# Tiles 4 and 5 of an attention turned by transposing DMAs and multiplied with the values in the banks of the gates

## The chip, the cores and the metric

The kernel runs on one core of one Trainium2 chip. The metric is the device time of one execution in microseconds (us). Before the change the median of 3 runs is 861.51 us (860.49 to 862.71).

## What is computed

```python
def reference(q, k, v, w_gate, w_val, w_out, w2_in, w2_out):
    # attention; keys and values are averaged in groups of 8 (576 -> 72)
    s = q @ mean8(k).T / sqrt(64)              # 4 batches, 8 heads, 576 queries
    x = softmax(s) @ mean8(v)                  # put together: 2304 x 512
    # gated layer, width 1536
    x = (sigmoid(x @ w_gate) * (x @ w_val)) @ w_out
    # second layer, width 2048
    h = x @ w2_in
    return (h * tanh(softplus(h))) @ w2_out    # 2304 x 512
```

All inputs are 64-bit floats in HBM. The kernel turns them into 32-bit floats itself, and multiplies matrices with three products of rounded halves (high by high, high by low, low by high).

## The kernel before, in words

**Blocks and parts.** The 2304 tokens are cut into blocks of 512, 512, 512 and 768. The first block of the gated layer, about the stretch from 55 to 140 us, is the one that matters here. Its loop runs over 12 slices of 128 of the hidden width (f = 0 to 11), and each slice has three *parts*: part 3f is the gate product (tile `pg`, L604 to L608), part 3f + 1 the value product (tile `pv`, same lines), part 3f + 2 the output product of the slice before (tiles `acc`, L123 to L125). So part 19 is the value product of slice 6, part 24 the gate product of slice 8, part 25 its value product, and part 26 the output product of slice 7.

**Banks.** `pg` and `pv` take turns in a pool of two PSUM banks ("mm"). A gate's bank is free when ScalarE has read it with a tanh (L954); a value's bank is free when VectorE has read it with `sg = (tanh + 1) * pv` (L960). Attention has another pool of two banks ("at").

**The table of small work.** Between two parts stand words of a table, START, written out by hand: the words after part k are recorded behind part k, on whatever engine they use. An engine takes its instructions in that order. The words after the block's parts do two things.
- They prepare the attention of the *next* block (tiles 4 to 7, 128 tokens each): scores (`m`), minimum (`M`), exponential (`X`, L465), normalising (`N`, L478 to L481), turning the weights of 128 tokens by 72 keys to 72 by 128 (8 heads), and the product with the pooled values.
- They convert the weights of the gated layer, 36 of them (24 of the gates and values, 12 of the output, `wo`): load (`raw_next`, L682), a scaling on ScalarE (`C`, L277), two bit operations on VectorE (`A`, L286 and L291), the rounded high half on ScalarE (`B`, L115) and the low half on GpSimd or VectorE (L310). Each `A` also issues the next load on SyncE.

**Two ways to turn a tile.** Tiles 4 and 5 are turned on TensorE: `t` makes 4 transposes in an "at" bank (L490), `c` copies them to SBUF on ScalarE or VectorE (L115 or L117), `p` multiplies with the values (L500), `h` and `l` split the product into halves (L514, L516), each of them for half of the heads at a time. Tiles 6 and later take the other way: `Y` clears a buffer `planes` on GpSimd (L547), `y` splits the 32-bit weights into two planes of 16-bit words on ScalarE (L553), a transposing DMA on SyncE's queue turns them (L559, tile `turned`), `j` joins the words again (four copies of ScalarE, L115), and `O` and `o` do the product with the values for all heads in one bank, with one rounding on ScalarE (L531) and one subtraction on VectorE (L532).

**Buffers.** `planes`, `turned` and the raw 64-bit weights of `wo` share one pool of three buffers ("raw"). The raw weights of gates and values have buffers of their own.

Of the kernel before, what the change touches and what calls it, by code (L numbers as in the profile page):

```python
# [26 lines left out]
E0.1 L1.0 B:a E1.1 C:a | A B:a A C:a |  |  | G:p B:a C:a K1.0:a A L1.2 C:a J1.0 B:a | A B:a G:p A  # L27
C:a | B:a C:a | C:a L1.3 A K1.1:a J1.1 B:a K1.2:a Z1.0:v | A A C:a J1.2 B:a B:a G:v Z1.1:v J1.3
K1.3:a C:a | A Z1.3:p | C:a A Z1.2:p | G:p B:d A B:a J1.4 C:a A m4.0 B:a | C:a | B:a M4.0 Q6 | A
m4.1 C:a | Z1.4:p X4.0 M4.1 G:v B:a F1 X4.1 C:a N4:v A C:a A H1 A B:a B:a | B:a C:a | A C:a t4.0 B:a  # L30
C:a | t4.1 | G:v A c4.0:a c4.1:v | A B:a | p4.0 p4.1 h4.1 h4.0 C:a G:v l4.0 l4.1 A B:a C:a B:a C:a A
| m5.0 A C:a B:a M5.0 m5.1 M5.1 X5.0 B:a Q7 X5.1 N5:p | A C:a B:a | G:v A | C:a B:d C:a | G:v t5.0
C:a A A c5.0:a | t5.1 B:a C:a c5.1:v A | B:a p5.0 A p5.1 B:a h5.0 l5.0 h5.1 l5.1 |  | m6.0 C:a M6.0
m6.1 A M6.1 X6.0 X6.1 G:v B:d C:a N6:v Y6 | A y6 B:a C:a m7.0 M7.0 m7.1 M7.1 X7.0:v X7.1:v | N7:v Y7
y7 A B:e G:p Q8 | B:a | Q9 j6.0 j6.1 | j7.0 j7.1:v G:v L2.0 L2.1 | O6 O7 o6 o7 | d m8.0 M8.0 m8.1
M8.1 | X8.0 X8.1 Q10 K2.0:v K2.1:v L2.2 L2.3 | r:a N8:v Y8 | s d y8 | b K2.2:v K2.3:v U2.0 U2.1 S0 |
r:a D0 | s d m9.0 M9.0 m9.1 M9.1 z0 | j8.0 b X9.0 X9.1 Q11 V2.0:p V2.1:v U2.2 U2.3 | j8.1 r:a N9:v
Y9 | s d y9 V2.2:p V2.3:v U2.4 U2.5 S1 | b D1 | r:a V2.4:p V2.5:v U2.6 U2.7 z1 | s d m10.0 M10.0
m10.1 M10.1 | j9.0 b X10.0 X10.1 Q12 V2.6:p V2.7:v | j9.1 r:a N10:v Y10 S2 | s d y10 D2 | O8 O9 b o8
o9 z2 | r:a | s d m11.0 M11.0 m11.1 M11.1 | j10.0 b X11.0 X11.1 Q13 S3 | j10.1 r:a N11:v Y11 L3.0  # L40
L3.1 D3 | s d y11 z3 | b | r:a K3.0:v K3.1:v L3.2 L3.3 | s d m12.0 M12.0 m12.1 M12.1 S4 | j11.0 b
X12.0 X12.1 Q14 D4 | j11.1 r:a N12:v Y12 K3.2:v K3.3:v U3.0 U3.1 z4 | s d y12 | b | O10 m13.0 M13.0
o10 m13.1 M13.1 O11 o11 r:a V3.0:p V3.1:v U3.2 U3.3 | s d | j12.0 b X13.0 X13.1 Q15 V3.2:p V3.3:v
U3.4 U3.5 S5 | j12.1 r:a N13:v Y13 D5 | s d y13 V3.4:p V3.5:v U3.6 U3.7 z5 | b S6 | r:a V3.6:p
V3.7:v D6 | j13.0 s d m14.0 M14.0 m14.1 M14.1 z6 | j13.1 b X14.0 X14.1 Q16 | r:a N14:v Y14 | s d y14
S7 | O12 O13 b D7 | r:a z7 | s d m15.0 M15.0 m15.1 M15.1 | j14.0 b X15.0 X15.1 Q17 | j14.1 r:a N15:v
Y15 S8 | s d y15 D8 | b z8 | r:a | s d m16.0 M16.0 m16.1 M16.1 | j15.0 b X16.0 X16.1 S9 | j15.1 r:a
N16:v Y16 D9 | s d y16 z9 | O14 O15 b | r:a | s d m17.0 M17.0 m17.1 M17.1 S10 | j16.0 b X17.0 X17.1
D10 | j16.1 r:a N17:v Y17 z10 | s d y17 | b | r:a S11 | s d D11 | j17.0 b z11 | j17.1 r:a | s d |
O16 O17 b | r:a x0.0 x0.1 x0.2 x0.3 x0.4 | s d x1.0 x1.1 x1.2 x1.3 x1.4 | b x0.5 x0.6 x0.7 x0.8 x0.9  # L50
x0.10 | r:a x1.5 x1.6 x1.7 x1.8 x1.9 x1.10 | s x0.11 | b x1.11 | x0.12 x0.13
"""

BIAS = 2.0**-112
# [3 lines left out]
def tile_pooled_attention_moe_mish(  # L58
# [14 lines left out]
    B, _, NPAIR, S = kt.shape  # L73
# [36 lines left out]
    def f32(ap):  # L110
        return ap.bitcast(F32)
# [15 lines left out]
    with tc.manual_schedule():  # L127
# [119 lines left out]
        with ExitStack() as actx:  # L247
# [10 lines left out]
            raw_q, scale_q, half_q = [], [], []  # L258
# [3 lines left out]
            def load_raw(src, eng=nc.sync, t=None):  # L262
                if t is None:
                    t = pa.tile([128, 512, 2], U32, tag="raw", name="raw", bufs=3)
                eng.dma_start(out=t.rearrange("p c w -> p (c w)"), in_=src.bitcast(U32))
                raw_q.append(t)

            def conv_scale(eng):

                raw = raw_q.pop(0)
                hi = f32(raw[:, :, 1])
                c = bits_at.pop(0) if bits_at else pa.tile([128, 512], U32, tag="cv", name="cv", bufs=3)
                if eng is nc.scalar:
                    eng.activation(out=f32(c), in_=hi, func=AF.Prelu, scale=BIAS, alpha=-(2.0**32))  # L277
                else:
                    eng.tensor_scalar_mul(f32(c), hi, BIAS)
                scale_q.append((raw, c, eng is nc.scalar))  # L280
# [149 lines left out]
            def ps_tile(tag, name):  # L430
                pool = {"mm": ps_mm, "at": ps_at}.get(tag, ps_acc)
                return pool.tile([128, 512], F32, tag=tag, name=name)
# [62 lines left out]
            def att_pv(T, g, tag="at", ps=None):  # L495
                ps = ps_tile(tag, "pv")[:, 0:256] if ps is None else ps
                for t0, n, b in segs(128 * T, 128):
                    for h in range(4 * g, 4 * g + 4):
                        p0, c0 = D * (h % 2), 128 * (h // 2 - 2 * g) + t0
                        nc.tensor.matmul(  # L500
                            ps[p0 : p0 + D, c0 : c0 + n],
                            vb_t[b][:, h, :],
                            pt_t[T][:, h, t0 : t0 + n],
                            start=True,
                            stop=True,
                        )
                pv_t[T, g] = ps.rearrange("p (a t) -> p a t", a=2)
# [9 lines left out]

            def att_values_out(T, j):

                ps = ps_tile("mm" if T in (10, 11) else "at", "pv")  # L520
                for g in range(2):
                    att_pv(T, g, ps=ps[:, 256 * g : 256 * g + 256])
                    del pv_t[T, g]
                t0 = 128 * T - blocks[j][0]
                if j == NBLK - 1:
                    c, t0 = divmod(t0, NG)
                    nc.scalar.copy(out=xs_t[0][:, :, c, t0 : t0 + 128], in_=ps.rearrange("p (k t) -> p k t", k=KD))
                    return lambda: None
                h, lo = (x[:, :, t0 : t0 + 128] for x in x_t[j % 2])
                ps = ps.rearrange("p (k t) -> p k t", k=KD)  # L530
                nc.scalar.copy(out=h, in_=ps)  # L531
                return lambda: nc.vector.tensor_sub(out=lo, in0=ps, in1=f32(h))  # L532
# [108 lines left out]
            with tc.tile_pool(name="pst", bufs=1, reuse_waits="tile") as pst:  # L641
# [29 lines left out]
                order = [("w", 0), ("w", 1), ("w", 2), ("w", 3), ("o", 0)]  # L671
                for f in range(NF):
                    if f + 2 < NF:
                        order += [("w", 2 * f + 4), ("w", 2 * f + 5)]
                    if f + 1 < NF:
                        order.append(("o", f + 1))
                pos = dict.fromkeys("lcab", 0)
                places = [
                    wpool.tile([128, 512, 2], U32, tag="w", name=f"wr{i}", bufs=2 * NF) for i in range(2 * NF)
                ]  # L680

                def raw_next(eng=nc.sync):  # L682
                    if pos["l"] < len(order):
                        kind, i = order[pos["l"]]
                        if kind == "o":
                            load_raw(wo[i], eng)
                        else:
                            load_raw((wg, wv)[i % 2][i // 2], eng, places[i])
                        pos["l"] += 1

                def scale_next(eng):
                    if pos["c"] < len(order):
                        conv_scale(eng)
                        pos["c"] += 1

# [219 lines left out]
            for j, (o, n) in enumerate(blocks[:-1]):  # L915
# [29 lines left out]
                for f in range(NF):  # L945
                    pg, pv = ((pre[f, nm] if j == 0 and f < 2 else None) for nm in "gv")
# [10 lines left out]
                    if pv is None:  # L957
                        pv = ps_mm.tile([128, 512], F32, tag="mm", name="pv")
# [76 lines left out]
            V, A = nc.vector, nc.scalar  # L1035
            for f in range(NF):
# [3 lines left out]
                a = pg_pool.tile([128, NG], F32, tag="sg", name="a", bufs=2)  # L1040
                u, v = (pg_pool.tile([128, NG], F32, tag="gh", name=t, bufs=2) for t in "uv")
                y = pg_pool.tile([128, NG], F32, tag="gl", name="y", bufs=2)

                def product(k):

                    pool, tag = banks1[k % 4]
                    ps = pool.tile([128, 512], F32, tag=tag, name=f"q{k}")
                    wt, c0 = where[k]
                    for kk in range(2):
                        xh, xl = pr[k, kk]  # L1050
                        mm3(ps[:, :NG], wt, slice(c0 + 128 * kk, c0 + 128 * kk + 128), xh, xl, kk == 0, kk == 1)
                    return ps[:, :NG]
# [10 lines left out]
                p5 = product(5)  # L1063
# [22 lines left out]
                p4 = product(4)  # L1086
# [96 lines left out]
        with ExitStack() as bctx:  # L1183
            pb = bctx.enter_context(tc.tile_pool(name="pb", bufs=1, reuse_waits="tile"))
            late = {f: pb.tile([128, NG], F32, name=f"g2_{f}") for f in range(6, NF2)}
            u0, v, a6, a7 = (pb.tile([128, NG], F32, name=t) for t in ("u", "v", "a6", "a7"))
# [57 lines left out]
            V, A, P = nc.vector, nc.scalar, nc.gpsimd  # L1244
# [75 lines left out]
            for p in range(NPR):  # L1320
                o = 2 * NG * p
# [5 lines left out]
                for i in range(NFP):  # L1327
# [12 lines left out]
                    a = a_at[i] if wino else a7  # L1340
# [170 lines left out]
                for j, (k, i) in enumerate(jobs[:-2]):  # L1511
# [7 lines left out]
                    if j in (8, 19):  # L1519
                        h = (8, 19).index(j)  # L1520
                        for t in range(NTG):
                            x = ob[t][:, half[h]]
# [100 lines left out]
```

## Time and profile before

| | |
|---|---|
| median of 3 runs | 861.51 us (860.49 to 862.71) |
| the profiled execution | 861.3 us |
| its span, first to last instruction | 859.3 us |
| mean granted clock of TensorE | 1.000 |
| TensorE busy | 850.5 us |
| VectorE, ScalarE, GpSimd busy | 627.6, 450.2, 143.9 us |

The profiled execution took 0.2 us less than the median, and 2 us of it lie outside the span. TensorE is busy nearly throughout; what another engine does counts where TensorE waits for it.

### The profile page before, as it was taken

Reading aid. Unit: us, or ns where it says so; the run is one execution under the profiler, and the core shown is the slowest. Engines: PE = TensorE matmul, PEld = TensorE weight load, DVE = VectorE, ACT = ScalarE, POOL = GpSimd, SP = SyncE. Lnnn points to the kernel's source line nnn. Section 1 sums busy time; section 2 is a strip of 40 time slices with the busy share of each in tenths; the row PEclk is TensorE's granted clock in tenths of the full one; section 3 lists DMA queues with packets and bytes.
Section 4 is the critical chain, followed back from the end, with each engine's and each line's share of the span. In section 5 each row is a group of like instructions: output and inputs, shape, how many; then the busy total and the mean of one; then the engine's idle time right before and its main releaser. Section 6 shows DMA issues by size and latency. Waiting matters only on the chain.

```text
span 859.3 us, 14411 instructions
## 1 busy us (share of the span) xinstructions
PE 850.5 (99%) x5044; PEld 780.3 (91%) x5044; DVE 627.6 (73%) x1181; ACT 450.2 (52%) x1067; POOL 143.9 (17%) x160
## 2 busy tenths in 40 slices
PE   8999999999999999999999999999999999999998
PEld 7887888888888888999999999998899999999998
DVE  6989774776675654778988977765577788566784
ACT  7656766554566544444454655555333466334454
POOL 3566431110120000010010024553000000000000
PEclk9999999999999999999999999999999999999999
DMA  9898537998889877165677789987598579776353
GB/s 339 308 309 270 157 114 235 285 265 248 274 211 290 233 213 258 62 221 196 226 241 235 277 316 330 349 286 270 180 293 293 184 224 315 258 238 226 120 191 99
DMA packets 117347, 207.02 MB, mean 241 GB/s; under 512 B 34972, under 2 KB 67740, under 8 KB 117276
## 3 DMA queue, kind: packets, MB, share of 16 engines
q1 hardware_dynamic: 116268, 204.12, 72.6%
q10 hardware_dynamic: 1008, 2.00, 0.7%
q8 instruction: 40, 0.66, 0.3%
q14 instruction: 31, 0.25, 0.1%
HBM read 143.80 MB, written 55.98 MB: 233 GB/s over the span
## 4 chain that ended last, share of the span: by engine, by line
PE 85%; DVE 6%; DMA 4%; ACT 3%; issue 2%; SPq 0%; ACTq 0%; DVEq 0%
PE acc L1218 8%; PE p L123 7%; PE p L125 7%; PE p L124 7%; PE x L1300 7%; PE acc L123 4%; PE acc L1300 4%; PE acc L125 4%; PE acc L124 4%; PE q L125 3%; PE q L123 3%; PE q L124 3%; PE pv L604 3%; PE pv L605 3%; PE pv L608 3%; PE pg L604 3%
## 5 line engine op out<-in xcount | busy, mean ns | idle before, releaser
L123 PE MATMUL p<-top,w2s 128*128 128x384 f32 x216 | 72.3, 335 | 0.0
L125 PE MATMUL p<-top,w2s 128*128 128x384 f32 x216 | 72.3, 335 | 0.0
L124 PE MATMUL p<-top,w2s 128*128 128x384 f32 x216 | 72.3, 335 | 0.0
L1218 PE MATMUL acc<-w,g 128*128 128x512 f32 x288 | 67.1, 390 | 0.0
L1218 PEld LDWEIGHTS acc<-w,g 128*128 128x128 f32 x288 | 53.9, 188 | 10.9
L123 PE MATMUL acc<-gh,wo 128*128 128x512 f32 x144 | 57.1, 396 | 0.0
L965 ACT CAST gh<-sg 128x512 fp32r<-128x512 f32 x36 | 22.3, 620 | 65.8 <-DVE sg L960 65.8
L124 PE MATMUL acc<-gl,wo 128*128 128x512 f32 x144 | 56.3, 391 | 0.0
L125 PE MATMUL acc<-gh,wo 128*128 128x512 f32 x144 | 56.1, 390 | 0.0
L1212 DVE TENSOR_TENSOR g<-g,g 128x384 fp32r<-128x384 f32 x64 | 35.9, 567 | 17.6 <-ACT g L1208 17.1
L1208 ACT CAST g<-g 128x384 fp32r<-128x384 f32 x64 | 32.4, 513 | 24.5 <-PE x L1300 13.9
L465 ACT ACTIVATE e<-sc,mx 128x72 f32<-128x72 f32 x136 | 41.3, 333 | 3.2 <-DVE mx L453 3.1
L123 PEld LDWEIGHTS p<-top,w2s 128*128 128x128 f32 x216 | 40.6, 188 | 0.4
L124 PEld LDWEIGHTS p<-top,w2s 128*128 128x128 f32 x216 | 40.6, 188 | 0.4
L125 PEld LDWEIGHTS p<-top,w2s 128*128 128x128 f32 x216 | 40.5, 188 | 0.0
L123 PE MATMUL p<-x1c,w2s 128*128 128x384 f32 x120 | 40.1, 334 | 0.0
L124 PE MATMUL p<-x1c,w2s 128*128 128x384 f32 x120 | 40.1, 334 | 0.0
L125 PE MATMUL p<-x1c,w2s 128*128 128x384 f32 x120 | 40.1, 334 | 0.0
L1370 ACT ACTIVATE g<-g 128x384 f32<-128x384 f32 x24 | 12.6, 525 | 49.1 <-DVE g L1358 49.1
L1096 POOL TENSOR_TENSOR g<-g,y 128x384 f32<-128x384 f32 x12 | 12.2, 1016 | 153.8 <-ACT g L1093 153.8
L1300 PE MATMUL acc<-w,g 128*128 128x256 f32 x288 | 37.3, 282 | 0.0
L1300 PE MATMUL x<-w2s,g 128*128 128x256 f32 x288 | 35.8, 284 | 1.0 <-DMA w2s<-td 1.0
(333 smaller groups left out, 2501.4 us busy)
## 6 DMA issues: line engine op xcount, KB each, us to landing
w2s<-wp SPq DMA_DIRECT2D x48, 512.0 KB
wo<-wod SPq DMA_DIRECT2D x39, 512.0 KB
wp<-w2s SPq DMA_DIRECT2D x24, 512.0 KB
raw<-w2i SPq DMA_DIRECT2D x16, 512.0 KB
raw<-w2o SPq DMA_DIRECT2D x16, 512.0 KB
w<-td SPq DMA_DIRECT2D x32, 256.0 KB
w2s<-td SPq DMA_DIRECT2D x32, 256.0 KB
wr<-wv SPq DMA_DIRECT2D x12, 512.0 KB
```

The source lines that it names most:

```text
L123: nc.tensor.matmul(ps, wt[:, 0, cols], xh, start=start, stop=False)
L124: nc.tensor.matmul(ps, wt[:, 0, cols], xl, start=False, stop=False)
L125: nc.tensor.matmul(ps, wt[:, 1, cols], xh, start=False, stop=stop)
L465: nc.scalar.activation(out=e_t[T][:, 4 * g + h, :], in_=s[:, h, :], func=AF.Exp, scale=-1.0, bias=mx_t[T][:, 4 * g + h, :], accum_out=sm_t ...
L604: nc.tensor.matmul(ps[:, c0:c1], w, xh[:, k, c0:c1], start=(k == 0), stop=False)
L605: nc.tensor.matmul(ps[:, c0:c1], w, xl[:, k, c0:c1], start=False, stop=False)
L608: nc.tensor.matmul(ps[:, c0:c1], w, xh[:, k, c0:c1], start=False, stop=(k == KD - 1))
L965: nc.scalar.copy(out=gh, in_=sg)
L1208: nc.scalar.copy(out=g[:, 0, :], in_=src)
L1212: nc.vector.tensor_sub(out=g[:, 1, :], in0=src, in1=f32(g[:, 0, :]))
L1218: nc.tensor.matmul(acc[t][0], g[:, a, c], w[:, b, :], start=(f == 0 and first), stop=(f == NF2 - 1 and last),)
L1300: nc.tensor.matmul(ps, g[:, a, c], rhs[b], start=start and a + b == 0, stop=stop and a == 1, skip_group_check=True)
```

## The change

Tiles 4 and 5 take the way of the later tiles: their `t`, `c`, `p`, `h`, `l` go, and `Y`, `y`, `j`, `O`, `o` come, in other places of the table. Tile 4 is split after part 16, joined after part 21 and multiplied after part 25; tile 5 is split after part 23, joined after parts 27 and 28 and multiplied after part 31. Their products with the values are put into an "mm" bank. Tile 5 is normalised on VectorE and one part later, and no more on GpSimd. Three roundings of weights (`B`) move from after part 14 to after part 15, behind the tanh of slice 5. Since two tiles now use the three "raw" buffers, the loads have an order of their own: raw `wo` of slices 6 to 11 come later, and the raw gates and values earlier.

```diff
@@ the table START, words after parts 14 to 31 @@
...
-m4.1 C:a | Z1.4:p X4.0 M4.1 G:v B:a F1 X4.1 C:a N4:v A C:a A H1 A B:a B:a | B:a C:a | A C:a t4.0 B:a
+m4.1 C:a | Z1.4:p X4.0 M4.1 G:v B:a F1 X4.1 C:a N4:v Y4 A C:a A H1 A | B:a B:a B:a C:a | A C:a B:a
...
@@ att_values_out @@
-                ps = ps_tile("mm" if T in (10, 11) else "at", "pv")
+                ps = ps_tile("mm" if T in (4, 5, 10, 11) else "at", "pv")
@@ the loads @@
+                raw_of = {}
+                loads = [x for x in order if x[0] == "w" or x[1] < 6]
+                for at, i in ((26, 6), (31, 7), (32, 8)):
+                    loads.insert(at, ("o", i))
+                loads += [None] * 2 + [("o", 9)] + [None] * 4 + [("o", 10), ("o", 11)]
...
                 def raw_next(eng=nc.sync):
-                    if pos["l"] < len(order):
-                        kind, i = order[pos["l"]]
+                    if loads:
+                        kind, i = loads.pop(0) or ("", 0)
                         if kind == "o":
                             load_raw(wo[i], eng)
-                        else:
+                        elif kind:
                             load_raw((wg, wv)[i % 2][i // 2], eng, places[i])
-                        pos["l"] += 1
+                        if kind:
+                            raw_of[kind, i] = raw_q.pop()
 
                 def scale_next(eng):
                     if pos["c"] < len(order):
+                        raw_q.insert(0, raw_of.pop(order[pos["c"]]))
                         conv_scale(eng)
                         pos["c"] += 1
```

Because of the added lines, lines from 676 on have numbers higher by 7 in the changed kernel (the tanh is L954 before and L961 after).

On **ScalarE**, between the scaling of the first weights of slice 9 and the tanh of slice 8 (`sg<-pg`, the last row of both pieces). Before:

```order
L277 ACTIVATE cv<-wr_250 128x512
L115 CAST wo<-cv 128x512
L465 ACTIVATE e,sm<-sc,mx 128x72 x4
L115 CAST wg_1263<-cv 128x512
L465 ACTIVATE e,sm<-sc,mx 128x72 x4
L965 CAST gh<-sg 128x512
L277 ACTIVATE cv<-raw 128x512
L115 CAST wv_1296<-cv 128x512
L954 ACTIVATE sg<-pg 128x512
```

In the changed kernel:

```order
L277 ACTIVATE cv<-wr_250 128x512
L115 CAST wo<-cv 128x512
L465 ACTIVATE e,sm<-sc,mx 128x72 x4
L115 CAST wg_1230<-cv 128x512
L465 ACTIVATE e,sm<-sc,mx 128x72 x4
L115 COPY pt<-turned 72x2x2x128 x4
L972 CAST gh<-sg 128x512
L277 ACTIVATE cv<-raw 128x512
L115 CAST wv_1270<-cv 128x512
L553 COPY planes<-e 128x8x72 x2
L961 ACTIVATE sg<-pg 128x512
```

The four copies that join tile 4 and the two that split tile 5 stand ahead of this tanh.

On **TensorE**, after the value product of slice 8 (part 25; its last products are the first row) and ahead of the output product of slice 7 (`acc`). Before:

```order
L608 MATMUL pv<-xh_229,wv_1214 128x512 x4
L490 MATMUL tr<-ident,e 72x128 x4
L123 MATMUL acc_750<-gh,wo 128x512
L124 MATMUL acc_750<-gl,wo 128x512
L125 MATMUL acc_750<-gh,wo 128x512
```

In the changed kernel:

```order
L608 MATMUL pv<-xh_229,wv_1183 128x512 x4
L500 MATMUL pv<-pt,vb 64x64 x16
L123 MATMUL acc_750<-gh,wo 128x512
L124 MATMUL acc_750<-gl,wo 128x512
L125 MATMUL acc_750<-gh,wo 128x512
```

Where the first half of tile 5 was turned, tile 4 is now multiplied with the values, in the bank that the gate product of slice 8 had.

On **SyncE**, the queue of the DMAs after parts 14 to 20 (`raw<-wo` is a load of raw output weights, `wod<-wo` a store of converted ones):

```order
 L389 DMA vb<-vpd 72x8x64
-L265 DMA wr_251<-wg 128x1024
-L595 DMA wod_76<-wo 128x1024
-L265 DMA wr_252<-wv 128x1024
-L265 DMA raw<-wo 128x1024
 L265 DMA wr_253<-wg 128x1024
 L265 DMA wr_254<-wv 128x1024
-L265 DMA raw<-wo 128x1024
+L595 DMA wod_76<-wo 128x1024
+L559 DMA_TRANSPOSE turned<-planes 128x16x128
+L265 DMA raw<-wo 128x1024 x2
 L595 DMA wod_77<-wo 128x1024
```

The raw output weights of slices 7 and 8 are now loaded behind the transposing DMA of tile 4.

## Rows read from the trace of the kernel before

**Rows 1.** The page, busy us of each engine (share of the span) and instructions.

```profile
PE 850.5 (99%) x5044; PEld 780.3 (91%) x5044; DVE 627.6 (73%) x1181; ACT 450.2 (52%) x1067; POOL 143.9 (17%) x160
```

**Rows 2.** Waits of PE from 55 to 140 us: total, times, longest us.

```profile
PE tr L490 <- DVE e L481: 0.6, 1, 0.6
```

**Rows 3.** Timeline of PE, parts 16 to 19: start us, us, instructions.

```profile
74.59 0.60 PE L490 MATMUL tr<-ident,e 128*72 128x128 f32 x4 [0.64 <-DVE e L481]
74.94 0.47 PE L123 MATMUL acc<-gh,wo 128*128 128x512 f32 x1
...
77.80 0.60 PE L490 MATMUL tr<-ident,e 128*72 128x128 f32 x4
78.15 0.47 PE L604 MATMUL pg<-xh,wg 128*128 128x512 f32 x1
...
80.98 0.39 PE L604 MATMUL pv<-xh,wv 128*128 128x512 f32 x1
```

**Rows 4.** Timeline of PE, after parts 20, 25 and 27.

```profile
86.51 1.15 PE L500 MATMUL pv<-pt,vb 72*64 72x64 f32 x32
87.59 0.50 PE L604 MATMUL pg<-xh,wg 128*128 128x512 f32 x1
...
102.33 0.60 PE L490 MATMUL tr<-ident,e 128*72 128x128 f32 x4
...
108.80 1.41 PE L500 MATMUL pv<-pt,vb 72*64 72x128 f32 x16
```

**Rows 5.** Timeline of DVE, up to its reading of the value product of slice 5.

```profile
76.48 1.51 DVE L286 TENSOR_SCALAR cv<-cv 128x512 uint32<-128x512 uint32 x1
78.03 1.65 DVE L291 SCALAR_TENSOR_TENSOR cv<-wr,cv 128x512 uint32<-128x512 uint32 x1
79.61 0.67 DVE L960 SCALAR_TENSOR_TENSOR sg<-sg,pv 128x512 f32<-128x512 f32 x1
```

**Rows 6.** Timeline of ACT: the tanhs of slices 6, 7, 8 (L954), what stands between.

```profile
83.92 0.58 ACT L954 ACTIVATE sg<-pg 128x512 f32<-128x512 f32 x1
...
89.42 0.67 ACT L277 ACTIVATE cv<-raw 128x512 f32<-128x512 f32 x1
...
92.59 0.57 ACT L954 ACTIVATE sg<-pg 128x512 f32<-128x512 f32 x1
...
101.36 0.59 ACT L954 ACTIVATE sg<-pg 128x512 f32<-128x512 f32 x1
```

**Rows 7.** Tile 6 through its transposing DMA: SPq, ACT and POOL timelines.

```profile
122.10 1.25 ACT L553 COPY planes<-e 128x576 uint16<-128x576 uint16 x2 [0.86 <-DVE e L481]
...
123.43 2.00 SPq L559 DMA_TRANSPOSE turned<-planes  x1
...
127.95 0.47 POOL L547 MEMSET planes<- 128x448 uint32 x1 [2.70 <-DMA turned<-planes]
...
130.62 2.64 ACT L115 COPY pt<-turned 72x512 uint16<-72x512 uint16 x4
```

**Rows 8.** All 12 transposing DMAs: ns on SyncE's queue, min/median/max, first and last.

```profile
L559 SPq DMA_TRANSPOSE turned<-planes x12: 1923/2528/4894, 123.4 to 315.8; - x12
```

**Rows 9.** One raw load, and windows: PE, PEld, DVE, ACT, POOL busy (x), clock, DMA, GB/s.

```profile
103.49 0.33 SPq L265 DMA_DIRECT2D raw<-wo  x1
...
104.00:106.00 2.00, 2.00 (x13) 1.65 (x12) 1.29 (x2) 1.22 (x4) 0.00 (x0) 1.00 0.78 127
106.00:108.00 2.00, 2.00 (x11) 1.66 (x10) 1.88 (x4) 1.22 (x4) 0.00 (x0) 1.00 0.98 359
```

**Rows 10.** The window between the tanhs of slices 7 and 8, columns as in Rows 9.

```profile
92.60:101.40 8.80, 8.80 (x40) 7.30 (x39) 5.84 (x11) 6.56 (x25) 4.72 (x4) 1.00 0.42 121
```

**Rows 11.** Waits of ACT from 72 to 102 us: total, times, longest us.

```profile
ACT cv L277 <- POOL wv L310: 0.5, 1, 0.5
...
ACT e L465 <- DVE mx L453: 0.2, 1, 0.2
```

More of the change, by code (lines that the diff above doesn't have):

```diff
@@ L29 @@
 K1.3:a C:a | A Z1.3:p | C:a A Z1.2:p | G:p B:d A B:a J1.4 C:a A m4.0 B:a | C:a | B:a M4.0 Q6 | A
-m4.1 C:a | Z1.4:p X4.0 M4.1 G:v B:a F1 X4.1 C:a N4:v A C:a A H1 A B:a B:a | B:a C:a | A C:a t4.0 B:a
-C:a | t4.1 | G:v A c4.0:a c4.1:v | A B:a | p4.0 p4.1 h4.1 h4.0 C:a G:v l4.0 l4.1 A B:a C:a B:a C:a A
-| m5.0 A C:a B:a M5.0 m5.1 M5.1 X5.0 B:a Q7 X5.1 N5:p | A C:a B:a | G:v A | C:a B:d C:a | G:v t5.0
-C:a A A c5.0:a | t5.1 B:a C:a c5.1:v A | B:a p5.0 A p5.1 B:a h5.0 l5.0 h5.1 l5.1 |  | m6.0 C:a M6.0
@@ L34 @@
[L34 to L48, printed above, removed]
@@ L49 @@
-D10 | j16.1 r:a N17:v Y17 z10 | s d y17 | b | r:a S11 | s d D11 | j17.0 b z11 | j17.1 r:a | s d |
-O16 O17 b | r:a x0.0 x0.1 x0.2 x0.3 x0.4 | s d x1.0 x1.1 x1.2 x1.3 x1.4 | b x0.5 x0.6 x0.7 x0.8 x0.9
-x0.10 | r:a x1.5 x1.6 x1.7 x1.8 x1.9 x1.10 | s x0.11 | b x1.11 | x0.12 x0.13
+m4.1 C:a | Z1.4:p X4.0 M4.1 G:v B:a F1 X4.1 C:a N4:v Y4 A C:a A H1 A | B:a B:a B:a C:a | A C:a B:a
+C:a y4 |  | G:v A | A B:a | C:a G:v A B:a C:a B:a C:a A | m5.0 A C:a B:a M5.0 m5.1 M5.1 X5.0 B:a Q7
+X5.1 j4.0 j4.1 | A N5:v Y5 C:a B:a | G:v A y5 | C:a B:d C:a | O4 G:v C:a A o4 A | B:a C:a A | B:a A
@@ new lines @@
+B:a j5.0 | j5.1 | m6.0 C:a M6.0 m6.1 A M6.1 X6.0 X6.1 G:v B:d C:a N6:v Y6 | A y6 B:a C:a m7.0 M7.0
+m7.1 M7.1 X7.0:v X7.1:v | O5 o5 N7:v Y7 y7 A B:e G:p Q8 | B:a | Q9 j6.0 j6.1 | j7.0 j7.1:v G:v L2.0
+L2.1 | O6 O7 o6 o7 | d m8.0 M8.0 m8.1 M8.1 | X8.0 X8.1 Q10 K2.0:v K2.1:v L2.2 L2.3 | r:a N8:v Y8 | s
+d y8 | b K2.2:v K2.3:v U2.0 U2.1 S0 | r:a D0 | s d m9.0 M9.0 m9.1 M9.1 z0 | j8.0 b X9.0 X9.1 Q11
+V2.0:p V2.1:v U2.2 U2.3 | j8.1 r:a N9:v Y9 | s d y9 V2.2:p V2.3:v U2.4 U2.5 S1 | b D1 | r:a V2.4:p
@@ new lines @@
+V2.5:v U2.6 U2.7 z1 | s d m10.0 M10.0 m10.1 M10.1 | j9.0 b X10.0 X10.1 Q12 V2.6:p V2.7:v | j9.1 r:a
+N10:v Y10 S2 | s d y10 D2 | O8 O9 b o8 o9 z2 | r:a | s d m11.0 M11.0 m11.1 M11.1 | j10.0 b X11.0
+X11.1 Q13 S3 | j10.1 r:a N11:v Y11 L3.0 L3.1 D3 | s d y11 z3 | b | r:a K3.0:v K3.1:v L3.2 L3.3 | s d
+m12.0 M12.0 m12.1 M12.1 S4 | j11.0 b X12.0 X12.1 Q14 D4 | j11.1 r:a N12:v Y12 K3.2:v K3.3:v U3.0
+U3.1 z4 | s d y12 | b | O10 m13.0 M13.0 o10 m13.1 M13.1 O11 o11 r:a V3.0:p V3.1:v U3.2 U3.3 | s d |
@@ new lines @@
+j12.0 b X13.0 X13.1 Q15 V3.2:p V3.3:v U3.4 U3.5 S5 | j12.1 r:a N13:v Y13 D5 | s d y13 V3.4:p V3.5:v
+U3.6 U3.7 z5 | b S6 | r:a V3.6:p V3.7:v D6 | j13.0 s d m14.0 M14.0 m14.1 M14.1 z6 | j13.1 b X14.0
+X14.1 Q16 | r:a N14:v Y14 | s d y14 S7 | O12 O13 b D7 | r:a z7 | s d m15.0 M15.0 m15.1 M15.1 | j14.0
+b X15.0 X15.1 Q17 | j14.1 r:a N15:v Y15 S8 | s d y15 D8 | b z8 | r:a | s d m16.0 M16.0 m16.1 M16.1 |
+j15.0 b X16.0 X16.1 S9 | j15.1 r:a N16:v Y16 D9 | s d y16 z9 | O14 O15 b | r:a | s d m17.0 M17.0
@@ L52 @@
+m17.1 M17.1 S10 | j16.0 b X17.0 X17.1 D10 | j16.1 r:a N17:v Y17 z10 | s d y17 | b | r:a S11 | s d
+D11 | j17.0 b z11 | j17.1 r:a | s d | O16 O17 b | r:a x0.0 x0.1 x0.2 x0.3 x0.4 | s d x1.0 x1.1 x1.2
+x1.3 x1.4 | b x0.5 x0.6 x0.7 x0.8 x0.9 x0.10 | r:a x1.5 x1.6 x1.7 x1.8 x1.9 x1.10 | s x0.11 | b
+x1.11 | x0.12 x0.13
 """
```

## The prediction

> **What bounds the kernel now.** I read the page's busy times first. TensorE (PE) is busy for 850.5 of 859.3 us [rows 1], so the change pays only where it takes work or a wait off PE, and costs only where it makes PE wait. The next view is PE's waits in the stretch of the change, the first block (55 to 140 us): there is one, 0.6 us, in front of the first transposes of tile 4, for its normalised weights [rows 2]. Everything else in this stretch is PE at work. So I then read the timelines of PE, VectorE (DVE) and ScalarE (ACT) side by side around parts 16 to 26, to see how far ahead of PE the readers of its two banks are. All times below are on the clock of the trace before.
>
> **What is taken off PE.** Four groups of transposes go. From the start of one to the start of the product behind it are 0.35 us, and that first product takes 0.47 us where the others take 0.39 [rows 3]: 0.43 us for a group, 1.7 us for four. The wait of 0.64 us in front of the first [rows 3] goes too, since tile 4 is needed much later. The products with the values only move: tile 4's (1.15 us) from after part 20 to after part 25, tile 5's (1.41 us) from after part 27 to after part 31 [rows 4]. Their count and shapes are the same, so they cost nothing net. Taken off: 1.7 + 0.64 = 2.4 us.
>
> **What PE gets back at once.** The value product of slice 6 (part 19) began at 80.98 [rows 3]. With two groups of transposes and the wait gone, PE is there at 80.98 - 0.64 - 0.86 = 79.5. But it needs the bank of the value product of slice 5, which DVE reads at 79.61 for 0.67 us, that is until 80.3 [rows 5]. Nothing ahead of this on DVE gets earlier: it is a run of conversions that begins with tile 4's exponentials, and the last of them are two operations of 1.51 and 1.65 us [rows 5]. So PE waits 0.8 us, a wait that stood hidden behind the transposes. What is left of the gain here is 0.7 us.
>
> **What ACT has to do more.** For a tile, two copies split it (1.25 us) and four join it (2.64 us) [rows 7]. Against this go one or two copies and roundings of some 0.6 us each, which ended in front of idle time and are worth nothing. ACT is not full on average (6.56 of 8.80 us between the tanhs of slices 7 and 8 [rows 10]), so what counts is what stands ahead of a tanh.
>
> *Tanh of slice 6.* It began at 83.92 [rows 6]. Tile 4's split is now right in front: 83.92 + 1.25 gives 85.2, its end 85.7. It frees the bank that the gate product of slice 7 wants: PE, 0.7 us early and without the product with tile 4's values (86.51 to 87.59 [rows 4]), is there at 86.5 - 0.7 = 85.8. It just fits.
>
> *The load behind the transposing DMA.* The DMA of tile 4 can be issued when the split ends, at 85.2, and holds SyncE's queue for 2.00 us as tile 6's did [rows 7]. Behind it stands the raw load of `wo` of slice 7: issued at 87.2. The nearest row for a load is the one issued at 103.49: its 512 KB are through by the bytes of the windows (254 KB up to 106, the rest at 359 GB/s) at some 106.8, 3.3 us later [rows 9]. So the scaling of that weight, which began at 89.42 [rows 6], can begin at 90.5 at best, or 90.9 with the bytes of the turned tile ahead. I take 90.7. Low bound of this wait: nothing, if the load overtakes; high bound: 3 us more, if SyncE needs 4.89 us for the DMA, its longest [rows 8]. What queues behind that scaling on ACT: two more weights, then the tanh of slice 7. ACT's earlier waits for DVE absorb the delay, and this tanh starts at about 92.3, where it started before (92.59 [rows 6]).
>
> *Tanh of slice 8.* From the tanh of slice 7 to the end of this one ACT had 6.56 us of work in 8.80 [rows 10]. Now the join of tile 4 and the split of tile 5 stand in between: 6.56 + 2.64 + 1.25 = 10.45 us. Of its idle time the waits for GpSimd's low half (0.5) and for the minimum (0.2) stay [rows 11]; the others were for results that will lie ready when ACT comes late. So it ends at 92.3 + 10.45 + 0.6 = 103.35; before it ended at 101.95 [rows 6], and PE did not need it then.
>
> **Where it is needed.** The product of tile 4 with the values takes the bank of the gate product of slice 8, straight after the value product of slice 8. So this tanh must be over one part earlier than before. That value product ended at 102.33, where tile 5's transposes began [rows 4]. With 0.7 us and the moved product (1.15) it ends at 100.45. PE then stands until 103.4: **2.95 us**. Behind PE's wait is all of its queue: the output product of slice 7, then slice 9. After this ACT and DVE are ahead of PE again. Tile 5's split ends by 102.8 and its DMA, at 4.5 us from issue to landing as for tile 6 (123.43 to 127.95 [rows 7]), lands near 107.3, well before its join after part 27. Its product with the values after part 31 needs a tanh that is done one part before, with no split or join in front of it.
>
> **Sum.** -2.4 + 0.8 + 2.95 = +1.4 us on the 861.3 us of the profiled execution: **862.7 us**. The median of the runs shown is 0.2 us above that execution; I leave it out. A measurement of this kernel tells about 0.3% (2.6 us) from no change, so my forecast is no difference that can be told.
>
> **A rule to weigh.** On the rows, four blocks cost PE 0.60 us of busy time [rows 3], and the DMA way 4.5 us until it lands plus 3.9 us of ACT [rows 7]. The Trainium skill (VectorE: DVE Perf Modes, Rules for kernel authors) says to turn a 128 by 128 block on TensorE where PSUM will do as destination, and by DMA otherwise; its section on the three transpose paths gives 390 ns against 1309 ns for a bf16 block. The trace agrees on which is the shorter, and by that rule alone the change loses wherever a turned tile is waited for. I put the latency at nothing, since the joins come five and four parts after the splits, and count ACT's copies instead; the rule speaks for the third rival.
>
> **Rivals.**
> - *Everything off PE stays off.* 861.3 - 2.4 = 858.9. For it: PE has one wait in this stretch [rows 2], and ACT is idle for a quarter of the window [rows 10]. Against: both banks named above, by 0.8 and 2.95 us. Chance 0.10.
> - *ACT is in time for tile 4's product, DVE is not for slice 6.* 861.3 - 1.6 = 859.7. ACT would have to gain 2.95 us on my walk: the raw load would have to be ready in time (worth 1 us), and the waits inside to vanish. Chance 0.12.
> - *The raw load comes later still, slower than before.* One mechanism: SyncE's queue. As long as the load of `wo` 7 lands by about 89.4 it costs nothing; I have 90.7; from 91 on each us goes through the scaling, the tanh of slice 7, ACT's chain and the tanh of slice 8 to PE. With the longest issue, 4.89 us in place of 2.00 [rows 8], it is 3 us: 865.7. For it: the median issue is 2.53 us [rows 8]. Against: the short ones are those with an idle DMA, as here, since the loads of gates and values are now over early. Chance 0.20.
> - *The turned tile itself is late.* Tile 4 lands by 89.7, its join comes at 97 or later: no.
>
> **How the numbers follow.** Forecast 0.58, with its own range 861 to 864 from 1 us either way at the tanh of slice 8; the first rival 0.10, the second 0.12, the third 0.20. The 80% range leaves out the first rival's end and the top of the third: 859.3 to 865.8. Faster by over 0.3% (below 858.9) takes the better half of the first rival: 0.06. Slower by over 0.3% (above 864.1) is the third rival and an edge of the forecast: 0.22. The rest, 0.72, is within 0.3%.
>
> **What would show it.** PE in the profile after: no L490 in this stretch beyond the start; a wait of about 0.8 us of the value product of slice 6 for DVE (L967); a wait of about 3 us of tile 4's product (L500) for ACT's tanh (L961). On ACT the scaling of a raw weight at about 90.7, waiting for a DMA. I am wrong if L500 does not wait for the tanh, if another part waits longer than it, or if the time leaves the range.

## The result, and the profile after

The changed kernel takes 866.26 us (median of 6 runs, 864.80 to 867.59) against 861.18 us for the kernel before (6 runs, 860.49 to 862.71). By the medians it is **5.1 us slower**; the ratio is 1.0065, with a 95% interval of 1.0050 to 1.0081. Forecast were 862.7 us, with a range from 859.3 to 865.8. A second batch gives 865.91 against 860.89 us, 1.0055 (1.0042 to 1.0068).

The profiled execution took 865.6 us; its span is 863.7 us, 4.4 us longer than before. The page's busy times, and its row of the granted clock in 40 slices:

```profile
PE 851.0 (99%) x5028; PEld 780.8 (90%) x5028; DVE 628.7 (73%) x1178; ACT 456.0 (53%) x1075; POOL 146.2 (17%) x161
...
PEclk9999899999999999999999999999999999999999
```

TensorE has 16 instructions fewer than in [rows 1] and is busy *longer*, by 0.5 us. The fifth slice of the clock says why: it is no longer full. The waits of PE from 55 to 140 us, which answer to [rows 2]:

```profile
PE pv L500 <- ACT sg L961: 3.9, 1, 3.9
```

The wait for tile 4's weights is gone, and one of 3.9 us has come, in the place and for the tanh that the prediction named. The timeline of PE from the value product of slice 6 (part 19) on, then around tile 4's product (L500) and up to the gate product of slice 9 (part 27), which answers to [rows 3, 4]:

```profile
79.08 0.41 PE L604 MATMUL pv<-xh,wv 128*128 128x512 f32 x1
...
98.63 1.07 PE L608 MATMUL pv<-xh,wv 128*128 128x512 f32 x4
103.62 1.98 PE L500 MATMUL pv<-pt,vb 72*64 72x64 f32 x32 [3.92 <-ACT sg L961]
105.53 0.80 PE L123 MATMUL acc<-gh,wo 128*128 128x512 f32 x1
106.12 0.63 PE L124 MATMUL acc<-gl,wo 128*128 128x512 f32 x1
...
109.96 0.61 PE L124 MATMUL acc<-gl,wo 128*128 128x512 f32 x1
110.39 0.41 PE L125 MATMUL acc<-gh,wo 128*128 128x512 f32 x1
110.64 0.40 PE L604 MATMUL pg<-xh,wg 128*128 128x512 f32 x1
```

Behind the wait everything is slow. From its start to the next instruction tile 4's product takes 1.91 us, where it took 1.08 [rows 4]. A product of 512 columns takes 0.63 us and not 0.39, and the output product of slice 7 takes 110.64 - 105.53 = 5.11 us; in the kernel before, that of slice 6 began at 94.17 and the part behind it at 96.89, 2.72 us. Then full speed is back. The windows view says what it is; columns are the stretch, its length, busy us of PE, PEld, DVE, ACT and POOL (with counts), the granted clock, the DMA share and GB/s:

```profile
84.00:86.00 2.00, 2.00 (x10) 1.66 (x9) 1.66 (x4) 1.25 (x4) 0.00 (x0) 1.00 0.40 100
86.00:88.00 2.00, 2.00 (x12) 1.69 (x11) 1.88 (x3) 1.55 (x3) 1.45 (x1) 1.00 1.12 216
...
99.50:103.60 4.10, 0.20 (x1) 0.00 (x0) 1.72 (x3) 4.10 (x9) 2.06 (x2) 1.00 0.00 0
103.60:110.60 7.00, 6.98 (x44) 5.82 (x45) 5.19 (x8) 4.03 (x8) 1.51 (x2) 0.51 0.98 201
110.60:114.00 3.40, 3.40 (x16) 2.80 (x16) 2.47 (x5) 0.99 (x2) 0.00 (x0) 1.00 0.38 129
```

While PE stands (99.5 to 103.6) ACT is busy for every one of the 4.1 us: it is the chain in front of the tanh. For the 7 us after that, the granted clock is 0.51, the lower of its two levels (1.2 GHz of 2.4). The Trainium skill (TensorE: Matmul & The Clock Gate, Part 1) says that the throttled clock is the default and that activity releases it; the trace agrees, with 1.00 until PE had stood for 3.9 us, 0.51 behind that, and 1.00 again after 7 us of work.

What ACT did, which answers to [rows 6], and the queue of SyncE:

```profile
82.85 1.23 ACT L553 COPY planes<-e 128x576 uint16<-128x576 uint16 x2
83.98 0.59 ACT L961 ACTIVATE sg<-pg 128x512 f32<-128x512 f32 x1
...
90.41 0.67 ACT L277 ACTIVATE cv<-raw 128x512 f32<-128x512 f32 x1 [2.85 <-DMA raw<-wo]
...
92.05 0.58 ACT L961 ACTIVATE sg<-pg 128x512 f32<-128x512 f32 x1
...
97.72 2.66 ACT L115 COPY pt<-turned 72x512 uint16<-72x512 uint16 x4
...
101.81 1.26 ACT L553 COPY planes<-e 128x576 uint16<-128x576 uint16 x2
102.96 0.61 ACT L961 ACTIVATE sg<-pg 128x512 f32<-128x512 f32 x1
```

```profile
84.10 1.89 SPq L559 DMA_TRANSPOSE turned<-planes  x1
86.05 1.14 SPq L265 DMA_DIRECT2D raw<-wo  x1
...
88.49 0.33 SPq L265 DMA_DIRECT2D raw<-wo  x1
```

The raw weight of `wo` 7 is issued at 86.05 and read at 90.41, so ACT waits 2.85 us for it, and the tanhs follow at 92.05 and 102.96. The load takes 4.36 us to its use, not the 3.5 of the prediction (3.3 from [rows 9], and 0.2). Its own issue holds the queue for 1.14 us, where that of the next load takes 0.33. From 86 to 88 us the DMA engines are full (a share of 1.12) and move only 216 GB/s, where [rows 9] have 359. The DMA view from the load's issue to 87.8 us says with what:

```profile
DMA packets 1454, 0.37 MB, mean 212 GB/s; under 512 B 1454, under 2 KB 1454, under 8 KB 1454
```

These are the turned tile's small packets, every one under 512 B. A load moves packets of 4 KB: the load of [rows 9] has its first at 0.96 us after its issue. Here the first comes at 1.77 us, when the turned tile is nearly through. So the load does not run beside the turned tile but behind it.

### The profile page after: what moved, and what is told of

Read it like the earlier page. It is cut to its first block, busy times and chain, and to the rows that moved or that the text cites. A ratio compares the mean times of both kernels' runs of the same rounds, so it can differ in the third digit from the quotient of the medians.

```text
span 863.7 us, 14382 instructions
## 1 busy us (share of the span) xinstructions
PE 851.0 (99%) x5028; PEld 780.8 (90%) x5028; DVE 628.7 (73%) x1178; ACT 456.0 (53%) x1075; POOL 146.2 (17%) x161
## 4 chain that ended last, share of the span: by engine, by line
PE 85%; DMA 5%; DVE 3%; ACT 3%; POOL 1%; issue 1%; SPq 0%; POOLq 0%; ACTq 0%; DVEq 0%
PE acc L1225 8%; PE x L1307 7%; PE p L123 7%; PE p L125 7%; PE p L124 7%; PE acc L123 4%; PE acc L1307 4%; PE acc L124 4%; PE acc L125 4%; PE q L125 3%; PE q L123 3%; PE q L124 3%; PE pg L604 3%; PE pv L605 3%; PE pg L608 3%; PE pv L604 3%
## 5 line engine op out<-in xcount | busy, mean ns | idle before, releaser
L123 PE MATMUL acc<-gh,wo 128*128 128x512 f32 x144 | 58.2, 404 | 0.0
L125 PE MATMUL acc<-gh,wo 128*128 128x512 f32 x144 | 56.9, 395 | 0.0
L967 DVE SCALAR_TENSOR_TENSOR sg<-sg,pv 128x512 f32<-128x512 f32 x34 | 23.2, 682 | 23.6 <-PE pv L608 23.2
L115 ACT COPY pt<-turned 72x512 uint16<-72x512 uint16 x54 | 37.5, 774 | 1.8 <-DMA turned<-planes 1.8
```

The lines of the kernel that those rows point to most:

```text
L115: eng.copy(out=out, in_=in_)
L123: nc.tensor.matmul(ps, wt[:, 0, cols], xh, start=start, stop=False)
L125: nc.tensor.matmul(ps, wt[:, 1, cols], xh, start=False, stop=stop)
```

## The experiments

Theory: the forecast's mechanism is right, and two prices were missing, the half clock behind the wait and the time for which the turned tile holds up the load. Rivals: the wait hangs on something else than this tanh, or the time is lost elsewhere. "Before" is always the kernel before in the same batch: 860.42 us (18 runs) for the first four, 860.59 (23 runs) for the next four, 860.89 (17 runs) for the last three.

**1. The bank alone.** Tile 4's product goes back to an "at" bank, and tile 5's with it.

```diff
-                ps = ps_tile("mm" if T in (4, 5, 10, 11) else "at", "pv")
+                ps = ps_tile("mm" if T in (10, 11) else "at", "pv")
```

> The changed kernel, but the products of tiles 4 and 5 with the values go back to the banks of attention. Theory (PE stands 3.9 us for the tanh of slice 8, because that bank is the gate's, and then runs 6.8 us at half clock): PE waits only for the join of tile 4, which ended at 100.2, so at most 0.9 us; no half clock; about 3.2 + 3.4 us less than the changed kernel, 859 to 860.5 us. Rival (the turning itself costs: ACT's copies and the DMA delay PE whatever the bank): the wait moves to another part and the time stays at 864 to 867 us.

Measured: 864.43 us, 1.0050 (1.0035 to 1.0065). L500 starts without a wait. PE's timeline:

```profile
100.07 1.44 PE L500 MATMUL pv<-pt,vb 72*64 72x64 f32 x32
...
118.93 0.76 PE L442 MATMUL sc<-kb,q 128*128 128x144 f32 x4 [2.12 <-ACT e L465]
```

So the "mm" bank is what tied the product to the tanh: this tanh was as late as ever (103.47). But ACT's lateness is still there, and PE meets it 19 us later, in the scores of tiles 6 and 7, whose exponentials ACT has not read (2.12 and 0.96 us). Behind these waits the clock is 0.51 for 3.5 us. Half of the theory and half of the rival: taking the reader away moves the wait.

**2. PE kept busy in the wait, too long.** 26 products of no use into an "at" bank ahead of tile 4's product; they are 52 instructions.

```diff
-| O4 G:v C:a A o4 A |
+| W26 O4 G:v C:a A o4 A |
```

> The changed kernel with 26 products of the identity with itself ahead of tile 4's product, to keep PE at work while it would wait. Theory (half of the loss is TensorE's clock, which falls because PE stands for 4 us): the tanh of slice 8 ends as late as before, about 103.5, but the granted clock stays at 1.00; 3 to 3.4 us less, 862.5 to 863.5 us. Rival (the clock falls for another reason, such as the transposing DMA that is issued at 103): clock 0.996 as in the changed kernel, 866 us or more.

Measured: 866.30 us, 1.0064 (1.0048 to 1.0081), and a granted clock of 1.00 throughout. The fill took 5.96 us and held L500 back to 106.92, 1.9 us after the tanh had ended. The clock is the theory's and the time the rival's. The run shows that work in the gap keeps the clock, not what that is worth. Runs 5 and 10 are the measurement.

**3. Tile 5's split behind the tanh of slice 8.**

```diff
-| G:v A y5 | C:a B:d C:a |
+| G:v A | y5 C:a B:d C:a |
```

> The changed kernel, but tile 5 is split one part later, behind the tanh of slice 8 on ACT. Theory (what stands ahead of that tanh on ACT sets PE's wait): the tanh is 1.15 us earlier and the wait 2.7 to 2.8 us; 865.0 us if the clock still falls for as long, 861.5 to 862 us if it does not. Rival (the tanh waits for something else): wait unchanged at 3.9 us, 866 us.

Measured: 863.26 us, 1.0034 (1.0020 to 1.0047). The tanh starts at 102.43, and PE's timeline and windows (columns as above) are:

```profile
103.10 1.15 PE L500 MATMUL pv<-pt,vb 72*64 72x64 f32 x32 [2.81 <-ACT sg L961]
```

```profile
103.10:110.00 6.90, 6.90 (x57) 5.74 (x58) 4.13 (x9) 5.04 (x9) 1.56 (x2) 1.00 0.66 163
```

The wait is 1.1 us shorter, for 1.25 us of copies moved, as the theory has it. In this trace the clock stays full, but the time is 1.3 us above what the theory gives for that: the scores now wait 1.0 us for ACT's exponentials, at 120.8 us. The nine executions show no price of the clock: the three with a mean clock of 1.000 took 862.4, 863.3 and 865.0 us, the two with 0.996 took 863.0 and 865.0.

**4. The load ahead of the transposing DMA.** Tile 4's split and DMA come after part 18.

```diff
-C:a y4 |  | G:v A |
+C:a |  | G:v A y4 |
```

> The changed kernel, but tile 4 is split two parts later, so that the raw load of wo of slice 7 stands ahead of the transposing DMA on SyncE. Theory (ACT stood 2.85 us for this load behind the DMA's issue of 1.9 us, and the delay went on to the tanh of slice 8): no wait of ACT for raw wo there, the tanh of slice 8 2 to 2.8 us earlier, PE's wait 1 to 2 us, no half clock: 859.5 to 861.5 us. Rival (the chain of join and split alone sets the tanh, the load wait is absorbed): the tanh under 0.7 us earlier, wait 3.3 us or more, time 865 to 866 us.

Measured: 862.86 us, 1.0031 (1.0019 to 1.0042). ACT's wait for the load is gone. On PE:

```profile
102.78 1.15 PE L500 MATMUL pv<-pt,vb 72*64 72x64 f32 x32 [2.45 <-ACT sg L961]
```

```profile
102.80:104.60 1.80, 1.80 (x35) 1.65 (x36) 0.77 (x2) 1.58 (x3) 0.12 (x1) 0.99 0.65 126
104.60:108.00 3.40, 3.40 (x9) 2.61 (x9) 2.68 (x5) 2.09 (x4) 0.00 (x0) 0.50 1.28 208
```

The wait is 1.45 us shorter, between the theory and the rival: counted from the start of part 19, the tanh ends 1.4 us earlier than in the changed kernel. 3.4 us at half clock are left: from L500 to part 27 are 5.53 us (102.78 to 108.31), where run 3 at full clock has 3.94. The ten executions don't all fall to the low clock: the three with a mean clock of 0.996 took 864.5 to 865.4 us, the two with 1.000 took 861.9 and 862.2. That is no price either, for the execution of this trace, with 0.997, took 861.8, and run 3 shows no such order.

**5. A shorter fill,** `W16` in place of `W26`, 32 instructions.

> The changed kernel with 16 short products of no use (into a free bank) ahead of tile 4's product with the values. By the durations of the longer fill (52 instructions in 5.96 us) these 32 take 3.7 us, about the 3.9 us for which TensorE stood. Theory (the miss is the clock behind the wait, the wait itself is as costly as forecast): the granted clock stays at full speed from 104 to 111 us, tile 4's product takes 1.15 us and still begins at about 103.6, and the time is 866.3 - 3.4 = 862.9 us. Rival (the wait or something else late in the program costs more than forecast, the clock is a side show): 865 us or more in spite of the full clock.

Measured: 864.05 us, 1.0040 (1.0028 to 1.0052), between the theory's 862.9 and the rival's 865. The fill takes 3.73 us and 0.36 us of wait are left (in this kernel and in run 10 the tanh is L963); the clock is 1.00. In this execution all of ACT is 1.5 us later than in the changed kernel's first trace (tanh of slice 6 at 85.47, where that has 83.98), and so is L500 (105.11 and 103.62).

**6. Both moves, 3 and 4.**

> Both single moves together: tile 4's split and transposing DMA after part 18 instead of 16, so that the load of raw output weights goes ahead of it, and tile 5's split after part 23's neighbour, behind the tanh of slice 8. Theory (ScalarE's chain to that tanh sets the wait, and its terms add): the two moves alone shortened the wait of tile 4's product by 1.45 and 1.1 us; together it is some 1.3 us, too short to show in the clock, tanh of slice 8 ends at about 101.6, and the time is 860.5 to 861 us. Rival (the terms don't add, since ScalarE then waits for GpSimd or VectorE instead, or a later wait for tile 5 takes the gain): the wait stays above 2 us or a new one of about 1 us stands at part 30, and the time is 862 to 863 us.

Measured: 861.98 us, 1.0019 (1.0008 to 1.0030). The wait is 1.27 us, as expected, and the clock 0.999, but PE also waits 1.0 us for DVE at part 19 and 1.0 us for the exponentials of the tiles after. The terms add; the time is 1 us above the theory's, for the waits that the rival named in general.

**7. Also tile 4's product one part later,** behind the output product of slice 7.

```diff
-| O4 G:v C:a A o4 A | B:a C:a A |
+| G:v C:a A A | O4 o4 B:a C:a A |
```

> As the run before, and tile 4's product with the values moved behind the output product of slice 7, 2.7 us later on TensorE. Theory (the loss was a deadline one part too early; with 2.7 us of slack nothing is left to wait for): tile 4's product begins without a wait at about 103, the granted clock stays full, and the time is 859 to 860 us, 1 us below the kernel before at best. Rival (another wait takes its place: the value product of slice 9 needs the bank that tile 4's product holds, and its two halves are taken late by ScalarE and VectorE, or the scores of tile 6 wait): a new wait of 1 to 2 us behind it, 861 us or more.

Measured: 861.38 us, 1.0010 (1.0001 to 1.0018). L500 has no wait, as both expected, and the rival is right on what follows. PE's waits:

```profile
PE pv L604 <- DVE x L532: 1.1, 1, 1.1
PE pg L604 <- DVE sg L967: 0.5, 1, 0.5
PE acc L124 <- DVE gl L817: 0.2, 1, 0.2
```

The bank with tile 4's product is emptied by DVE (L532) behind two conversions, and PE wants it.

**8. The kernel before, a second trace.**

> The kernel before once more, for a second trace of it. Theory (VectorE's lead of 1.4 us from about 55 us on in the changed kernel's trace is due to when one transfer landed in that execution, not to the change): here the reading of slice 5's value product on VectorE begins anywhere between 78.2 and 79.7 us, and TensorE's wait for tile 4's weights is between 0 and 0.7 us. Rival (the change moved it): both within 0.1 us of the first trace, 79.61 and 0.64.

Measured: a span of 857.4 us. There is no wait for tile 4's weights, and DVE reads slice 5's values at 78.72, where [rows 5] have 79.61. DVE's wait for pooled values from HBM near 55 us (`vs`) is 0.29 us here, 1.69 in the first trace of before and 0.35 in the first of after. So the lead of DVE in the changed kernel's first trace needs no effect of the change: it moves from execution to execution, and that transfer is a part of it. The prediction's wait of 0.64 us, too, is there in one execution and not in the other.

**9 and 10. The changed kernel and the fill of 32 instructions again, on one chip.**

> The changed kernel once more, beside the next one on the same chip, for its time and a second trace. Theory (two terms were missing from the sum: 3.4 us of half clock, and 0.9 us by which the raw load shares the DMA engines with the transposing DMA): 4.3 to 6 us above the kernel before; tile 4's product waits 3.8 to 4.1 us for the tanh, and the output product behind it runs at half clock, 5.1 us instead of 2.7. The raw load needs 4.3 to 4.4 us from its issue to the scaling that reads it. Rival (the first trace was a lucky or unlucky single case): a wait under 3 us, or a full clock, in this trace.

> The 16 short products ahead of tile 4's product once more, beside the changed kernel on the same chip, to measure what the clock alone costs in the time and not only in one trace. Theory: 3 to 3.4 us below the changed kernel of this batch. Rival (the clock's loss is partly made up later, where TensorE would have waited anyway): 1.5 to 2.2 us below, as the two batches so far give (1.0065 against 1.004 of before).

Measured: 865.91 us, 1.0055 (1.0042 to 1.0068), and 864.03 us, 1.0038 (1.0026 to 1.0050). The second trace of the changed kernel is of its slowest execution (869.46 us). PE's timeline:

```profile
81.22 0.47 PE L604 MATMUL pv<-xh,wv 128*128 128x512 f32 x1 [1.41 <-DVE sg L967]
...
105.81 1.97 PE L500 MATMUL pv<-pt,vb 72*64 72x64 f32 x32 [3.90 <-ACT sg L961]
107.71 0.80 PE L123 MATMUL acc<-gh,wo 128*128 128x512 f32 x1
...
112.80 0.39 PE L604 MATMUL pg<-xh,wg 128*128 128x512 f32 x1
```

That of the fill:

```profile
100.15 3.73 PE L662 MATMUL warm<-ident 128*128 128x128 f32 x32
104.23 1.15 PE L500 MATMUL pv<-pt,vb 72*64 72x64 f32 x32 [0.34 <-ACT sg L963]
105.31 0.50 PE L123 MATMUL acc<-gh,wo 128*128 128x512 f32 x1
...
108.19 0.39 PE L604 MATMUL pg<-xh,wg 128*128 128x512 f32 x1
```

From L500 to the gate product of slice 9 are 6.99 us at half clock and 3.96 with the fill: 3.0 us on the spot. The raw load was issued at 88.25 and read at 92.59, 4.34 us again. The medians differ by 1.9 us, as the rival said. All six executions of the changed kernel (864.64 to 869.46) are slower than all five with the fill (863.39 to 864.57), so the gain is real; its size is not settled by so few. Neither trace has a later wait of PE in this block in which the rest could be made up. PE's times from the start of part 16 to that of part 35, by the traces:

| trace | part 16 | part 35 | between |
|---|---|---|---|
| before, first and second | 71.07, 71.07 | 131.34, 130.53 | 60.3, 59.5 |
| changed, first and second | 70.92, 71.49 | 135.66, 137.81 | 64.7, 66.3 |
| fill, runs 5 and 10 | 71.88, 71.75 | 134.43, 133.51 | 62.6, 61.8 |

In this stretch the fill gives back 2.2 to 4.6 us. The rest of the span differs by up to 3 us from one of the thirteen traces to another (797.9 to 801.2 us), whatever the kernel. That scatter is as large as the price that is sought; how much of the 3.0 us reaches the end stays open.

**11. Run 7 with DVE freed.** Tile 5's split goes behind the roundings after part 24, and two conversions of DVE behind the subtraction that empties tile 4's bank.

```diff
-| y5 C:a B:d C:a | G:v C:a A A | O4 o4 B:a C:a A |
+| C:a B:d C:a y5 | G:v C:a | O4 o4 A A B:a C:a A |
```

> The run with tile 4's product a part later, with the two waits behind it taken away: tile 5's split is put behind the roundings after part 24, so that VectorE's low half of an output weight and the reading of slice 8's value product come earlier, and two conversions of VectorE go behind the subtraction that frees tile 4's bank. Theory (TensorE's 0.5 us for the bank of slice 8's values and 1.1 us for tile 4's bank are what is left of the loss): neither wait shows, and the time is 1.5 us less, 859 to 860 us, some 0.7 to 1 us below the kernel before. Rival (the 1.6 us only moves to the next reader, the tanh of slice 9 or the scores of tile 6): 861 us or more, with a new wait of 1 us or more between 105 and 125 us.

Measured: 861.65 us, 1.0019 (1.0008 to 1.0030). Both waits of run 7 are gone, and PE's timeline has new ones:

```profile
117.30 0.76 PE L442 MATMUL sc<-kb,q 128*128 128x144 f32 x4 [0.60 <-ACT e L465]
119.01 0.76 PE L442 MATMUL sc<-kb,q 128*128 128x144 f32 x4 [0.95 <-ACT e L465]
```

The rival was right: 1.55 us of waits, where 1.6 were taken away. The scores of tiles 6 and 7 wait for ACT, as in runs 1, 3 and 6. No version beats the kernel before; the best, runs 7 and 11, have medians 0.8 us above it.

## Why the prediction failed

*The place was right.* The transposes and their wait are gone, and tile 4's product waits for the tanh of slice 8, the longest wait of the stretch. ACT's walk, on the first trace: scaling of `wo` 7 at 90.41 (forecast 90.7), tanh of slice 7 at 92.05 (92.3), end of that of slice 8 at 103.57 (103.35).

*The step that failed is the sum.* It counted the wait as 2.95 us of standing and let all of PE's queue go on behind it at full speed. There was no term for the clock, and no reason for leaving it out. With the forecast's start of L500 at 103.4, 1.08 us for it and 2.72 for the output product, part 27 begins at 107.2; it began at 110.64. Of these 3.4 us, 0.2 are the start, 0.8 are L500 and 2.4 the output product at half clock: **3.2 us for the clock**, on the spot. The runs with PE kept busy show it by itself: clock 1.00, and 3.0 us less from L500 to part 27. All of the forecast's windows had a clock of 1.00 [rows 9, 10], and it added a 3 us gap to them without asking what a gap does.

*The second term, the load, was mis-sized by 0.9 us.* "I take 90.7" rested on 3.3 us from [rows 9] and 0.2 for the turned tile. The load of [rows 9] was not alone: a load of queries and two stores were issued from 103.91 to 104.86, so the bytes of those windows are theirs too. Here it took 4.36 us, and 4.34 in the second trace. 0.8 of the 0.9 lie ahead of its first packet (1.77 us after the issue, not 0.96): the load stands behind the turned tile, for which the forecast had 0.2. Its issue on SyncE is longer by 0.8 us as well (1.14 and 0.33), so these traces don't tell whether the queue or the DMA engines held it; no run has the one without the other. That 90.41 came out near 90.7 is luck: DVE, and with it tile 4's split, was over 1 us ahead in that execution. In the second trace, without that lead, the same steps come at 92.59, 94.26 and 105.75.

In both traces PE waits 3.9 us and not 2.95. That this difference is as large as the load's 0.9 is luck too. From tile 4's split to the end of the tanh of slice 8 ACT took 20.7 us and not 19.4: 0.9 of it is the load, and 0.5 lies behind the tanh of slice 7, where the wait for GpSimd was 0.8 and not 0.5. Against that, PE took 20.6 us and not 20.2 from part 19 to the end of part 25.

*The wait of 0.8 us at part 19* is 0 in the first trace and 1.41 in the second, 0.56, 0.3 and 1.0 in runs 2, 5 and 6, and 0 in the others. It is real, and its size moves with DVE's lead. The transfer near 55 us is only a part of that: DVE waited 0.93 us for it in the second trace and 0.35 in the first, but was 1.3 us later already ahead of it (49.71 and 48.45). The wait adds in full: PE stands as long before L500 where it is 1.41 (3.90) as where it is 0 (3.92).

*The sum, mended:* 1.4 + 0.9 + 3.2 = 5.5 us, against 5.1 and 5.0 measured. This agreement shows less than it seems to. With the clock kept (runs 5 and 10) 3.5 and 3.1 us of loss are left, where the mended sum leaves 2.3, and the fill gave back 1.9 us by the medians of run 10's batch, not 3.2. That the clock and the wait make the loss is shown; how it divides, to within 1 us, is not.

*The rivals.* The first two needed a tanh of slice 8 in time for tile 4, and PE waited 3.9 us for it. The third, a later load, has the right direction and comes near in time (865.7 us), but not by its mechanism: the transposing DMA took 1.89 us to issue, less than the 2.00 assumed, and the load itself was late. Its argument from an idle DMA does not hold: the DMA share was 0.70 from 82 to 84 us, just ahead of this short issue. The rule that the prediction weighed gave the right sign: four groups of transposes are worth 1.7 us here (2.4 with the wait in front of the first), and even with the clock full and the wait gone (run 7) the other way is 0.8 us slower (0.1 to 1.5 by the interval); what PE then waits for, in runs 1, 3, 6 and 11, is ACT, which has the 3.9 us of copies for each tile.

## What to carry to other kernels

A wait of the engine that bounds the kernel costs its length and what follows: when a forecast puts several us of standing on TensorE, price the work behind it at both levels of the granted clock. A load that was issued behind a transposing DMA moved nothing until the turned tile was nearly through (1.8 us here); take its time from a stretch that has both. And when small work is moved in front of a reader that PE needs, taking that reader away (other bank, later place) may only show the next one: runs 1, 7 and 11 freed one wait and met others of 1.5 to 3 us in all.

## What was not expected of the hardware

How long PE stands does not alone decide the clock here. In the trace of run 3 it stayed at 1.00 after 2.81 us; in that of run 4 it fell to 0.50 after 2.45 us, not at once but 1.8 us into the work, for 3.4 us; in that of run 1 it fell behind two waits of 2.12 and 0.96 us. The same kernel does both: in runs 3 and 4 mean clocks of single executions go from 0.996 to 1.000. After 3.9 us (the changed kernel) it was half at once, for 7 us, and the mean clock was 0.995 to 0.998 in all twelve executions. So a wait of some 2.5 us cost its length alone in one trace and 1.6 us more in another, and repeating a run is needed to know which.
